# Second head group of a gated convolution: x written by TensorE once, five taps on ScalarE and VectorE, in batches 1 to 6

## Chip, cores and metric

The kernel runs on one core of a Trainium2 chip. The metric is the device time of one launch in microseconds (us). The engines are TensorE (PE; its weight loads are listed apart as PEld), VectorE (DVE), ScalarE (ACT), GpSimd (POOL) and SyncE (SP, which issues the DMAs). PSUM is where TensorE writes; DVE and ACT read it.

## What is computed

Eight batches. In each, eight heads attend to 32 memory slots that are made from k, v and phi; the result, with the heads laid side by side as x (576 rows, 512 channels), goes through a gated convolution.

```python
a = softmax(phi, axis=seq)                       # 576 x 32 weights for each head
k_m, v_m = a.T @ k, a.T @ v                      # 32 x 64 each
attn = softmax(q @ k_m.T / 8, axis=slots)        # 576 x 32
x = attn @ v_m                                   # heads side by side: 576 x 512
gate = sigmoid(sum(conv_w[i] * shift(x, 4 - i) for i in range(5)))   # for each channel
out = (gate * (x @ w_val)) @ w_out
```

## The kernel before, in words

Channels lie on the partitions and sequence positions along the rows, in two halves s of 288 positions. The heads form two groups g of four. The 512 channels are four tiles t of 128; group 0 owns t = 0 and 1, group 1 owns t = 2 and 3. Products against w_val and w_out are made of a high and a low part of each operand (vwH, vwL, pH, pL, hH, hL, woH, woL), three matmuls for each pair.

The steps of one batch b, each a function of that name: `phi_max`, `phi_turn`, `phi_top`, `phi_diag`, `phi_spread`, `phi_lay`, `phi_sub`, `phi_exp` make the softmax over the sequence; `slots`, `slots_inv`, `slots_scale`, `slots_turn`, `slots_place` the memory slots; `scores`, `scores_turn` the scores (PSUM to `st`); `soft_max`, `soft_sub`, `soft_exp`, `soft_sum`, `soft_inv`, `soft_mul` the softmax over the slots; `soft_turn` turns it into `pT`, `soft_high` and `soft_low` split it into pH and pL; `val_rows`, `val_high`, `val_low`, `val_again` fold w_val into the slots' values. `taps(b, g)` multiplies the slots' values by the five tap weights. `conv(b, g)` (L557) multiplies `pT` by these on TensorE, five shifted readings accumulated in PSUM, for both halves and four heads: 40 matmuls with 32 rows and 64 columns of weights, which gives the gate of two channel tiles before the sigmoid. `sigmoid(b, t)` (L572) writes the gate to SBUF. `value(b, s, t)` (L579) makes one channel tile of x @ w_val in six products, `gated(b, s, t)` (L590) multiplies it by the gate into h, `gated_high` and `gated_low` split h, `project(b, s, n)` (L610) makes an output tile in twelve products, `place` copies it out of PSUM, `store` writes it to memory.

In the second half of the positions `conv` puts the heads' channels one place further in the array ("swapped" channels), so that value and project read weights shifted by 64 channels there: `val_again` and `wo_pair` make these copies.

The order of all steps is the text `ORDER` (L38), one word for each step, read from left to right; each engine runs its own instructions in that order and waits for the data of others. A star after a word takes the other of two engines for that step (`pick`, L191): for `phi_sub`, `soft_sub`, `soft_mul`, `soft_low` POOL without a star and DVE with one, for `soft_high` and `gated_high` ACT without and DVE with, for `taps` and `gated_low` POOL without and DVE with.

PSUM is shared out through two pools: four buffers `b` of one bank, for all products but two, and two buffers `cv` of two banks, for `scores`, `conv` and the filler matmuls `warm` at the start. A buffer is written again when its last reader is done.

Of the kernel before, what the change touches and what calls it, by code (L numbers as in the profile page):

```python
# [42 lines left out]
narrow_bits.v.2 narrow_sign.v.2 narrow_size.v.1 narrow_sign.v.0 narrow_round.v.3 narrow_done.v.1 narrow_add.v.0
narrow_round.v.2 narrow_bits.v.3 load_q.0.0 narrow_add.v.2 narrow_sign.v.3 narrow_size.v.0 narrow_size.v.2
narrow_done.v.0 narrow_add.v.3 load_w.o.0 slots.0.0 warm.4 narrow_done.v.2 narrow_size.v.3 load_phi.0.1 slots_inv.0.0
narrow_done.v.3 slots_scale.0.0* load_w.o.1 slots_turn.0.0 taps.0.0* slots_place.0.0 scores.0.0 warm.7 narrow_bits.o.0
narrow_round.o.0 narrow_sign.o.0 load_kv.0.1 phi_max.0.1 narrow_add.o.0 scores_turn.0.0 phi_turn.0.1 warm.7
narrow_round.o.1 soft_max.0.0 narrow_size.o.0 phi_top.0.1 soft_sub.0.0 narrow_bits.o.1 phi_diag.0.1* phi_spread.0.1
warm.9 phi_sub.0.1* load_q.0.1 soft_exp.0.0 soft_sum.0.0 phi_exp.0.1 narrow_done.o.0 load_phi.1 slots.0.1 warm.5
narrow_sign.o.1 wo_high.0 soft_inv.0.0 wo_low.0 slots_inv.0.1 load_w.o.2 soft_mul.0.0* slots_scale.0.1* narrow_add.o.1  # L50
slots_turn.0.1 soft_turn.0.0 slots_place.0.1 val_rows.0 load_w.o.3 soft_high.0.0 phi_max.1 taps.0.1 narrow_size.o.1
scores.0.1 val_high.0.1 soft_low.0.0 load_kv.1.0 scores_turn.0.1 phi_turn.1 val_high.0.0 narrow_round.o.2 soft_max.0.1
conv.0.0 val_again.0.1.vwH val_again.0.0.vwH* phi_top.1 soft_sub.0.1 narrow_round.o.3 val_low.0.0 phi_diag.1*
val_low.0.1 val_again.0.0.vwL soft_exp.0.1 narrow_bits.o.2 phi_spread.1 val_again.0.1.vwL soft_sum.0.1 sigmoid.0.0
load_kv.1.1 soft_inv.0.1 soft_mul.0.1* phi_lay.1 sigmoid.0.1 soft_turn.0.1 phi_sub.1* conv.0.1 soft_high.0.1 load_q.1
soft_low.0.1* phi_exp.1 narrow_bits.o.3 narrow_sign.o.3 value.0.1.2 narrow_sign.o.2 narrow_add.o.3 value.0.0.0
sigmoid.0.2 narrow_done.o.1 value.0.0.1 narrow_add.o.2 slots.1.0 load_phi.2 gated.0.0.0 wo_high.1 gated.0.1.2
gated.0.0.1 narrow_size.o.3 slots.1.1 wo_low.1 slots_inv.1.0 gated_high.0.0.0 wo_pair.0.0 narrow_done.o.3
narrow_size.o.2 value.0.1.0 gated_low.0.0.0 slots_scale.1.0* value.0.0.2 sigmoid.0.3 slots_inv.1.1 gated.0.1.0
wo_pair.1.0 wo_high.3 value.0.0.3 narrow_done.o.2 slots_scale.1.1* wo_low.3 gated.0.0.2 slots_turn.1.0 wo_high.2  # L60
slots_turn.1.1 gated.0.0.3 value.0.1.3 slots_place.1.0 wo_pair.0.1 gated_high.0.0.1* slots_place.1.1 wo_low.2
scores.1.0 gated.0.1.3 scores.1.1 scores_turn.1.0 gated_low.0.0.1 val_rows.1 gated_high.0.1.1 wo_pair.1.1
scores_turn.1.1 value.0.1.1 val_high.1.0 soft_max.1 gated_low.0.1.1 project.0.0.0 val_high.1.1 val_again.1.0.vwH*
load_kv.2.0 val_low.1.0 val_again.1.1.vwH taps.1.1 gated.0.1.1 project.0.0.2 place.0.0.0 val_low.1.1 gated_high.0.1.0
val_again.1.0.vwL soft_sub.1* val_again.1.1.vwL gated_low.0.1.0 project.0.0.1 place.0.0.2 phi_max.2 soft_exp.1
project.0.1.2 load_kv.2.1 taps.1.0* project.0.1.0 place.0.0.1 soft_sum.1 place.0.1.2 project.0.1.3 soft_inv.1
soft_mul.1* store.0.0.0 project.0.1.1 place.0.1.3 soft_turn.1 store.0.1.1 phi_turn.2 load_q.2 soft_high.1* conv.1.0
place.0.1.0 place.0.1.1 phi_top.2 soft_low.1 phi_diag.2* phi_spread.2 sigmoid.1.0 project.0.0.3 load_phi.3 value.1.1.1
phi_lay.2 place.0.0.3 phi_sub.2* value.1.1.0 sigmoid.1.1 store.0.0.1 value.1.0.0 gated.1.1.0 phi_exp.2 store.0.1.0
value.1.0.1 gated.1.1.1 gated.1.0.0 value.1.1.2 gated.1.0.1 phi_max.3 conv.1.1 gated_high.1.1.0 gated_high.1.0.0  # L70
gated_low.1.1.0 slots.2.0 gated_low.1.0.0 sigmoid.1.2 slots.2.1 slots_inv.2.0 load_kv.3.0 sigmoid.1.3 gated.1.1.2
value.1.1.3 slots_scale.2.0* slots_inv.2.1 taps.2.0* slots_scale.2.1* value.1.0.2 gated.1.1.3 taps.2.1 phi_turn.3
gated_high.1.1.1 gated.1.0.2 value.1.0.3 phi_top.3 gated_low.1.1.1 slots_turn.2.1 phi_diag.3* gated.1.0.3
slots_turn.2.0 load_kv.3.1 slots_place.2.1 phi_spread.3 gated_high.1.0.1* slots_place.2.0 scores.2.1 phi_lay.3
gated_low.1.0.1 scores.2.0 phi_sub.3* val_rows.2 project.1.0.0 val_high.2.0 val_high.2.1 val_again.2.0.vwH*
val_again.2.1.vwH load_q.3 val_low.2.0 project.1.1.2 phi_exp.3 val_low.2.1 val_again.2.0.vwL scores_turn.2.0
val_again.2.1.vwL project.1.1.0 scores_turn.2.1 place.1.1.2 place.1.0.0 soft_max.2 project.1.1.3 place.1.1.0
load_phi.4 soft_sub.2* project.1.0.1 place.1.1.3 soft_exp.2 store.1.1.1 project.1.0.3 place.1.0.1 soft_sum.2
store.1.0.0 project.1.0.2 soft_inv.2 soft_mul.2* slots.3.1 place.1.0.2 place.1.0.3 soft_turn.2 store.1.0.1 slots.3.0
soft_high.2* conv.2.1 load_kv.4.0 slots_inv.3.1 soft_low.2 slots_inv.3.0 slots_scale.3.1* phi_max.4 slots_scale.3.0*  # L80
slots_turn.3.0 sigmoid.2.2 slots_turn.3.1 project.1.1.1 taps.3.1 load_kv.4.1 value.2.0.2 slots_place.3.0
slots_place.3.1 sigmoid.2.3 scores.3.0 gated.2.0.2 val_rows.3 place.1.1.1 scores_turn.3.0 phi_turn.4 val_high.3.1
conv.2.0 phi_top.4 val_high.3.0 val_again.3.1.vwH val_low.3.1 phi_diag.4* val_low.3.0 store.1.1.0 val_again.3.1.vwL
val_again.3.0.vwH* val_again.3.0.vwL value.2.0.3 taps.3.0* sigmoid.2.0 value.2.0.1 sigmoid.2.1 gated.2.0.3
gated_high.2.0.1* value.2.1.2 gated_low.2.0.1 value.2.0.0 gated.2.1.2 value.2.1.3 gated.2.0.0 gated.2.0.1 scores.3.1
gated.2.1.3 gated_high.2.0.0 phi_spread.4 load_q.4 scores_turn.3.1 gated_high.2.1.1 gated_low.2.0.0 value.2.1.1
soft_max.3 phi_lay.4 value.2.1.0 gated_low.2.1.1 project.2.0.2 soft_sub.3* gated.2.1.0 project.2.0.1 soft_exp.3
load_phi.5 gated.2.1.1 phi_sub.4* project.2.0.0 gated_high.2.1.0 soft_sum.3 place.2.0.2 gated_low.2.1.0 project.2.0.3
phi_exp.4 soft_inv.3 place.2.0.0 project.2.1.1 place.2.0.3 soft_mul.3* place.2.0.1 store.2.0.0 project.2.1.0
soft_turn.3 store.2.0.1 project.2.1.2 soft_high.3* place.2.1.0 place.2.1.1 store.2.1.0 phi_max.5 conv.3.0 soft_low.3  # L90
place.2.1.2 slots.4.1 sigmoid.3.0 value.3.0.1 slots_inv.4.1 value.3.0.0 slots_scale.4.1* sigmoid.3.1 taps.4.1
value.3.0.2 gated.3.0.0 gated.3.0.1 conv.3.1 gated_high.3.0.0 gated_low.3.0.0 slots.4.0 sigmoid.3.2 sigmoid.3.3
gated.3.0.2 value.3.1.0 slots_inv.4.0 load_kv.5.0 slots_scale.4.0* value.3.1.2 gated.3.1.0 taps.4.0* value.3.1.3
gated.3.1.2 project.2.1.3 gated.3.1.3 gated_high.3.1.1 gated_low.3.1.1 value.3.0.3 place.2.1.3 store.2.1.1
slots_turn.4.0 gated.3.0.3 phi_turn.5 slots_place.4.0 slots_turn.4.1 gated_high.3.0.1* value.3.1.1 load_kv.5.1
slots_place.4.1 phi_top.5 gated_low.3.0.1 scores.4.0 gated.3.1.1 phi_diag.5* scores.4.1 scores_turn.4.0
gated_high.3.1.0 phi_spread.5 gated_low.3.1.0 scores_turn.4.1 project.3.0.0 phi_lay.5 soft_max.4 project.3.1.2
# [580 lines left out]
```

## Time and profile before

| what | value |
|---|---|
| median of three runs | 285.92 us (285.54 to 287.08) |
| the profiled execution | 287.87 us |
| its span, first to last instruction | 286.1 us |
| PE busy | 272.5 us, 95% of the span |
| DVE, ACT, POOL busy | 194.7, 148.8, 107.8 us |
| the chain of work that ended last, by engine | PE 83%, DVE 8%, DMA 4% |

The span is what the rows below divide up; the profiled execution is 1.77 us longer than its span, and 1.95 us longer than the median of the runs.

### The profile page before, as it was taken

Reading aid. Unit: us, or ns where it says so; the run is one execution under the profiler, and the core shown is the slowest. Engines: PE = TensorE matmul, PEld = TensorE weight load, DVE = VectorE, ACT = ScalarE, POOL = GpSimd, SP = SyncE. Lnnn points to the kernel's source line nnn. Section 1 sums busy time; section 2 is a strip of 40 time slices with the busy share of each in tenths; the row PEclk is TensorE's granted clock in tenths of the full one; section 3 lists DMA queues with packets and bytes.
Section 4 is the critical chain, followed back from the end, with each engine's and each line's share of the span. In section 5 each row is a group of like instructions: output and inputs, shape, how many; then the busy total and the mean of one; then the engine's idle time right before and its main releaser. Section 6 shows DMA issues by size and latency. Waiting matters only on the chain.

```text
span 286.1 us, 8415 instructions
## 1 busy us (share of the span) xinstructions
PE 272.5 (95%) x3682; PEld 233.2 (82%) x3682; DVE 194.7 (68%) x287; ACT 148.8 (52%) x262; POOL 107.8 (38%) x96
## 2 busy tenths in 40 slices
...
GB/s 222 353 382 377 309 224 37 134 273 236 322 64 332 266 164 321 10 257 126 165 7 351 157 185 235 89 247 309 183 113 42 32 2 44 82 85 45 41 84 84
DMA packets 13237, 50.00 MB, mean 175 GB/s; under 512 B 1672, under 2 KB 2184, under 8 KB 10256
## 3 DMA queue, kind: packets, MB, share of 16 engines
...
q14 instruction: 8, 0.07, 0.1%
...
## 4 chain that ended last, share of the span: by engine, by line
PE 83%; DVE 8%; DMA 4%; SPq 2%; ACT 1%; issue 0%; POOL 0%; ACTq 0%
PE b L615 34%; PE b L585 17%; PE cv L565 14%; PE b L392 7%; PE cv L438 3%; PE cv L206 2%; DMA raw<-in_w_val_dram 2%; PE b L522 2%; DMA kv<-in_kv_dram 2%; PE b L364 1%; DVE hH L261 1%; DVE hH L254 1%; PE b L422 1%; SPq L313 1%; DVE w_val_sb L286 1%; PE b L336 1%
## 5 line engine op out<-in xcount | busy, mean ns | idle before, releaser
L615 PE MATMUL b<-hL,woH 128*128 128x288 f32 x256 | 76.1, 297 | 0.8 <-DMA kv<-in_kv_dram 0.7
L615 PE MATMUL b<-hH,woL 128*128 128x288 f32 x256 | 75.5, 295 | 0.0
L615 PE MATMUL b<-hH,woH 128*128 128x288 f32 x256 | 75.5, 295 | 0.0
L199 POOL TENSOR_TENSOR hL<-h,hH 128x576 fp32r<-128x576 f32 x32 | 47.1, 1476 | 66.2 <-ACT hH L196 46.0
L594 DVE TENSOR_TENSOR h<-b,gate 128x288 f32<-128x288 f32 x64 | 28.0, 453 | 42.6 <-PE b L585 35.7
L196 ACT COPY o<-b 128x288 f32<-128x288 f32 x64 | 24.6, 399 | 54.9 <-PE b L615 52.9
L615 PEld LDWEIGHTS b<-hL,woH 128*128 128x128 f32 x256 | 48.1, 188 | 3.8 <-POOL hL L199 1.8
L615 PEld LDWEIGHTS b<-hH,woL 128*128 128x128 f32 x256 | 48.1, 188 | 0.0
L615 PEld LDWEIGHTS b<-hH,woH 128*128 128x128 f32 x256 | 48.1, 188 | 0.0
L565 PE MATMUL cv<-pT,taps 32*64 32x288 f32 x1280 | 45.0, 418 | 2.4 <-DVE pT L498 2.4
L565 PEld LDWEIGHTS cv<-pT,taps 32*64 32x64 f32 x1280 | 29.0, 135 | 13.7 <-issue 5.2
L199 POOL TENSOR_TENSOR pL<-pT,pH 128x1152 fp32r<-128x1152 f32 (+1 forms) x8 | 20.9, 2619 | 42.9 <-DVE pH L196 21.5
L585 PE MATMUL b<-pL,vwH 128*128 128x288 f32 x128 | 28.9, 307 | 0.5 <-DVE h L594 0.5
L585 PE MATMUL b<-pH,vwL 128*128 128x288 f32 x128 | 27.3, 295 | 0.0
L585 PE MATMUL b<-pH,vwH 128*128 128x288 f32 x128 | 27.3, 295 | 0.0
L574 ACT ACTIVATE gate<-cv 128x576 f32<-128x576 f32 x32 | 20.2, 652 | 13.5 <-PE cv L565 13.4
L196 ACT CAST hH<-h 128x576 fp32r<-128x576 f32 x24 | 15.9, 672 | 18.9 <-DVE h L594 14.6
L585 PEld LDWEIGHTS b<-pL,vwH 128*128 128x128 f32 x128 | 20.1, 188 | 5.3 <-issue 2.1
L392 PE MATMUL b<-kv,e 128*32 128x129 f32 (+1 forms) x640 | 22.8, 277 | 0.1
L206 PE MATMUL cv<-ident 128*128 128x128 f32 x142 | 20.7, 308 | 1.4 <-POOL ident masks.py:199 1.4
L206 PEld LDWEIGHTS cv<-ident 128*128 128x128 f32 x142 | 19.6, 221 | 2.7 <-POOL ident masks.py:199 1.4
L392 PEld LDWEIGHTS b<-kv,e 128*32 128x32 f32 (+1 forms) x640 | 15.6, 108 | 7.4 <-issue 6.7
...
## 6 DMA issues: line engine op xcount, KB each, us to landing
...
```

The source lines that it names most:

```text
L196: eng.copy(out=out, in_=x) if eng is nc.scalar else eng.tensor_copy(out=out, in_=x)
L199: eng.tensor_tensor(out=out, in0=x, in1=hi.bitcast(F32), op=ALU.subtract)
L206: nc.tensor.matmul(ps[:, i % 2, 0:P], lhsT=ident, rhs=ident, start=True, stop=True)
L254: nc.vector.tensor_scalar(out=a.bitcast(I32), in0=raw[:, :, 1], scalar1=3, scalar2=0x3FFFFFF8, op0=ALU.logical_shift_left, op1=ALU.bitwise ...
L392: nc.tensor.matmul(km[j * M:(j + 1) * M, 0:2 * D + 1], lhsT=e[0:n, g, c, j * M:(j + 1) * M], rhs=x[0:n, c, j, :], start=(c == 0), stop=(c ...
L438: nc.tensor.matmul(sc[j * M:(j + 1) * M, s, 0:HALF], lhsT=live["kvT", b, g][rows, 0, j * M:(j + 1) * M], rhs=live["q", b][rows, g, j, :], ...
L522: nc.tensor.matmul(ps[g][j * M:(j + 1) * M], lhsT=live["kvT", b, g][rows, 1, j * M:(j + 1) * M], rhs=w_val_sb[rows, j, :], start=True, sto ...
L565: nc.tensor.matmul(cv[t][x * D:(x + 1) * D, s, 0:HALF], lhsT=w[rows, i, :], rhs=p[rows, g, s * HALF + i:(s + 1) * HALF + i], start=(i == 0 ...
L574: nc.scalar.activation(out=gt, in_=live["cv", b, t][:, :, 0:HALF], func=AF.Sigmoid)
L585: nc.tensor.matmul(vp[:, 0:HALF], lhsT=a[:, t // PG, n:n + P], rhs=p[:, g, s * HALF:(s + 1) * HALF], start=(i == 0), stop=(i == len(parts) ...
L594: nc.vector.tensor_tensor(out=live["h", b, s, y][:, i], in0=live["vp", b, s, t][:, 0:HALF], in1=live["gate", b, t][:, s], op=ALU.mult)
L615: nc.tensor.matmul(ps[:, 0:HALF], lhsT=w[:, t, n * P:(n + 1) * P], rhs=a[:, t % 2], start=(i == 0), stop=(i == len(parts) - 1))
```

## The change

For group 1 in batches 1 to 6, `conv` and `taps` go. `keep_v` copies the slots' values into a taps tile without multiplying, and `mix` lets TensorE write x itself, for 292 positions of each half (four of them before it), into both `cv` buffers: 8 matmuls in place of 40. `tap(b, t, i)` then makes the convolution from PSUM: i = 0 on ACT (multiply by a weight for each partition, into the gate tile), i = 1 to 4 on DVE (multiply and add into the gate tile, 128 partitions by 576 elements each). `open_gate` is the sigmoid in place. The weights for each partition, `cwP`, are made once by `turn_taps` (10 small matmuls) and `lay_taps`. For that group the channels are no longer moved in the second half, so `val_again` copies half as much, and `value` and `project` read the unshifted weights.

`ORDER` is another text throughout. Counted over it: `phi_sub` of batches 1 to 7 is on POOL where it was on DVE, `soft_high` on ACT where it was on DVE in seven batches, `gated_high` on ACT where DVE had eight of them, all `taps` on POOL, one `place` of each batch on DVE; the filler matmuls are 61, not 71; the loads of w_val's fourth and w_out's tiles come later, those of kv earlier; in batch 7 both convolutions come one after the other at the end of batch 6's projections.

```diff
+VECTOR_CONV = {1, 2, 3, 4, 5, 6}
...
+    def swapped(b, g):
+        return g != G - 1 or b not in VECTOR_CONV
...
+    @step
+    def turn_taps(_):
+        ps = psum.tile([P, 512], F32, name="b", bufs=BUFS["b"])
+        ps = ps[:, 0:KT * PG].rearrange("p (k t) -> p k t", k=KT)
+        for x in range(2):
+            for i in range(KT):
+                nc.tensor.matmul(ps[x * D:(x + 1) * D, i], lhsT=cw_sb[:, 0, i * D:(i + 1) * D],
+                                 rhs=ident[0:H, H - HG + x:H:2], start=True, stop=True)
+        live["cwT"] = ps
+
+    @step
+    def lay_taps(_):
+        high(nc.scalar, cwP, live["cwT"])
...
     def val_again(b, g, n):
+        gs = slice(0, G if swapped(b, G - 1) else G - 1)
         x = live[n, b, g].bitcast(F32)
-        high(pick(nc.gpsimd, nc.scalar), live[n, b, g][:, :, HG * D:], x[:, :, 0:D])
+        high(pick(nc.gpsimd, nc.scalar), live[n, b, g][:, gs, HG * D:], x[:, gs, 0:D])
...
+    @step
+    def keep_v(b):
+        w = work.tile([P, KT, D], F32, name="taps", bufs=BUFS["taps"])
+        high(pick(nc.gpsimd, nc.scalar), w[:, 0], live["kvd", b, G - 1][:, 1, 0])
+        live["taps", b, G - 1] = w
+
+    @step
+    def mix(b):
+        cv = [psum.tile([P, 2, 512], F32, name="cv", bufs=BUFS["cv"]) for _ in range(PG)]
+        for s in range(2):
+            for j in range(HG):
+                rows = slice(j * M, (j + 1) * M)
+                t, x = divmod(j, 2)
+                nc.tensor.matmul(cv[t][x * D:(x + 1) * D, s, 0:PAD + HALF], lhsT=live["taps", b, G - 1][rows, 0, :],
+                                 rhs=pTs[b % 2][rows, G - 1, s * HALF:(s + 1) * HALF + PAD], start=True, stop=True)
+        for j in range(PG):
+            live["cv", b, NP - PG + j] = cv[j]
+
+    @step
+    def tap(b, t, i):
+        x, w = live["cv", b, t][:, :, i:i + HALF], cwP[:, i, t - (NP - PG):t - (NP - PG) + 1]
+        if i == 0:
+            gt = work.tile([P, 2, HALF], F32, name="gate", bufs=BUFS["gate"])
+            nc.scalar.activation(out=gt, in_=x, func=AF.Identity, scale=w)
+            live["gate", b, t] = gt
+        else:
+            gt = live["gate", b, t]
+            nc.vector.scalar_tensor_tensor(out=gt, in0=x, scalar=w, in1=gt, op0=ALU.mult, op1=ALU.add)
+
+    @step
+    def open_gate(b, t):
+        gt = live["gate", b, t]
+        nc.scalar.activation(out=gt, in_=gt, func=AF.Sigmoid)
...
-            n = t % PG * P + s * D
+            n = t % PG * P + (s * D if swapped(b, t // PG) else 0)
...
-        parts = [(w[s], live[a, b, s, t // 2], t) for t in range(NP)
+        parts = [(w[s if swapped(b, t // PG) else 0], live[a, b, s, t // 2], t) for t in range(NP)
                  for w, a in ((woH, "hL"), (woL, "hH"), (woH, "hH"))]
```

**TensorE, around the second group's convolution of batch 2.** L615 (L676 after the change) is project, L392 slots, L565 conv, L611 mix, L422 (L447) slots_turn, L361 phi_turn. Before:

```order
L615 MATMUL b<-hH,woH_83 128x288
L392 MATMUL b<-kv,e 32x129 x40
L565 MATMUL cv<-pT_74,taps 64x288 x40
L422 MATMUL b<-ident,kvd 128x128 x4
L615 MATMUL b<-hL,woH_84 128x288
L615 MATMUL b<-hH,woL_86 128x288
```

In the changed kernel:

```order
L676 MATMUL b<-hH,woH_84 128x288
L611 MATMUL cv<-pT_74,taps 64x292 x8
L361 MATMUL b<-ident,mx 128x128 x2
L447 MATMUL b<-ident,kvd 128x128 x2
L676 MATMUL b<-hL,woH_84 128x288
L676 MATMUL b<-hH,woL_86 128x288
```

The 40 matmuls have become 8, and phi_turn of batch 4, which needs phi_max of batch 4 from DVE, now stands right behind them.

**VectorE, after the softmax of batch 2.** L322, L324 and L325 (L347, L349, L350) are phi_max of batch 4, L594 (L655) gated, L447 (L472) scores_turn, L343 (L368) phi_top, L199 val_low, L550 taps; L207 is here a place and L625 the taps. Before:

```order
L322 TENSOR_TENSOR mx<-e 128x2x2x128
L324 TENSOR_TENSOR mx<-mx 128x256
L325 TENSOR_TENSOR mx<-mx,e 64x256
L594 TENSOR_TENSOR h<-b,gate 128x288
L447 STREAM_TRANSPOSE st<-cv 128x576
L343 TENSOR_REDUCE top<-b 128x2
L199 TENSOR_TENSOR vwL<-b,vwH 128x2x256 x2
L550 TENSOR_TENSOR taps<-cwB,kvd 128x320
```

In the changed kernel:

```order
L347 TENSOR_TENSOR mx<-e 128x2x2x128
L349 TENSOR_TENSOR mx<-mx 128x256
L350 TENSOR_TENSOR mx<-mx,e 64x256
L207 COPY o<-b 128x288
L368 TENSOR_REDUCE top<-b 128x2
L625 SCALAR_TENSOR_TENSOR gate<-cv,cwP,gate 128x576 x8
L655 TENSOR_TENSOR h<-b,gate 128x288 x8
L472 STREAM_TRANSPOSE st<-cv 128x576 x2
```

Eight taps stand between phi_top and the eight gated of batch 2, and all of them ahead of the scores of batch 3.

**GpSimd, batches 1 and 2.** L199 (L210) is soft_low where it writes pL and gated_low where it writes hL, L550 (L576) taps, L196 (L207) val_again, L402 phi_sub. Before:

```order
L199 TENSOR_TENSOR pL<-pT_76,pH 128x1152
L550 TENSOR_TENSOR taps<-cwB,kvd 128x320
L199 TENSOR_TENSOR hL<-h,hH 128x576 x4
L199 TENSOR_TENSOR pL<-pT_74,pH 128x1152
L196 CAST vwH<-vwH 128x2x64
L196 CAST vwL<-vwL 128x2x64 x2
```

In the changed kernel:

```order
L210 TENSOR_TENSOR pL<-pT_74,pH 128x1152
L576 TENSOR_TENSOR taps<-cwB,kvd 128x320
L210 TENSOR_TENSOR hL<-h,hH 128x576 x4
L402 TENSOR_TENSOR e<-e,mxa 128x1280
L207 CAST vwL<-vwL 128x64 x2
L210 TENSOR_TENSOR pL<-pT_76,pH 128x1152
```

phi_sub, which was DVE's, now stands in POOL's queue between gated_low and the next soft_low.

## Rows read from the trace of the kernel before

**Rows 1.** Busy time in two stretches (columns in its first line)

```profile
core 0: us, PE busy (x) PEld busy (x) DVE busy (x) ACT busy (x) POOL busy (x), PEclk, DMA share, GB/s
...
100.00:130.00 30.00, 30.00 (x437) 25.14 (x436) 24.36 (x35) 15.41 (x30) 10.84 (x9) 1.00 0.51 181
220.00:253.00 33.00, 33.00 (x459) 28.33 (x458) 18.75 (x29) 15.05 (x28) 11.33 (x10) 1.00 0.12 46
```

**Rows 2.** The chain of work that ended last: start us, us, what (L565 conv)

```profile
41.90 4.47 PE cv L565 x80
...
71.67 0.22 PE b L336 x2
71.88 2.61 PE cv L565 x80
74.50 0.64 PE b L364 x4
...
88.87 0.44 PE b L422 x4
...
90.08 1.13 PE cv L438 x32
91.21 0.86 PE b L522 x16
...
109.33 1.59 PE b L615 x12
110.91 0.79 PE b L585 x6
...
136.96 1.37 PE b L392 x40
```

**Rows 3.** Groups by line: shapes, xcount, busy us, mean ns, idle before

```profile
L574 ACT ACTIVATE gate<-cv 128x576 f32<-128x576 f32 x32 | 20.2, 652 | 13.5 <-PE cv L565 13.4
...
L199 DVE TENSOR_TENSOR vwL<-b,vwH 128x512 fp32r<-128x512 f32 x16 | 10.4, 682 | 5.3 <-ACT vwH L196 5.3
...
L411 ACT ACTIVATE kvd<-b,ri 128x256 f32<-128x256 f32 x16 | 7.6, 475 | 13.9 <-DVE ri L401 13.7
...
L196 ACT COPY kvT<-b 128x256 f32<-128x256 f32 x16 | 5.4, 372 | 3.2 <-PE b L422 3.1
```

**Rows 4.** DVE's phi_max of batches 6 and 7: start us, us, engine, line

```profile
164.90 0.68 DVE L322 TENSOR_TENSOR mx<-e 128x512 f32<-128x512 f32 x1
165.62 2.76 DVE L324 TENSOR_TENSOR mx<-mx 128x256 f32<-128x256 f32 x1
168.41 0.42 DVE L325 TENSOR_TENSOR mx<-mx,e 64x256 f32<-64x256 f32 x1
...
199.76 0.43 DVE L324 TENSOR_TENSOR mx<-mx 128x256 f32<-128x256 f32 x1
```

**Rows 5.** DVE from scores_turn to soft_turn of batch 5, columns as rows 4

```profile
183.60 1.45 DVE L447 STREAM_TRANSPOSE st<-cv 128x576 f32<-128x576 f32 x2 [0.68 <-PE cv L438]
...
186.64 1.34 DVE L462 TENSOR_REDUCE mm<-st 128x36 f32<-128x1152 f32 x1
...
188.26 1.37 DVE L469 TENSOR_TENSOR st<-st,mm 128x1152 f32<-128x1152 f32 x1
190.87 1.35 DVE L480 TENSOR_REDUCE ss<-st 128x36 f32<-128x1152 f32 x1 [1.24 <-ACT st L474]
...
192.88 1.36 DVE L493 TENSOR_TENSOR st<-st,ss 128x1152 f32<-128x1152 f32 x1
194.27 1.38 DVE L498 STREAM_TRANSPOSE pT<-st 128x1152 f32<-128x1152 f32 x1
```

**Rows 6.** POOL's soft_low of batch 4, columns as rows 4

```profile
165.06 3.04 POOL L199 TENSOR_TENSOR pL<-pT,pH 128x1152 fp32r<-128x1152 f32 x1 [10.85 <-DVE pH L196]
```

**Rows 7.** PE's clock before and in the convolution of batch 0, columns as rows 1

```profile
40.00:42.00 2.00, 0.10 (x2) 0.13 (x5) 1.93 (x4) 1.83 (x5) 0.00 (x0) 1.00 0.01 5
42.00:44.00 2.00, 2.00 (x36) 2.00 (x43) 2.00 (x3) 1.97 (x3) 0.00 (x0) 0.52 0.00 0
```

More of the change, by code (lines that the diff above doesn't have):

```diff
@@ L43 @@
[L43 to L97, printed above, removed]
@@ new lines @@
+warm.9 soft_sub.0.0* phi_sub.0.1* soft_exp.0.0 load_q.0.1 soft_sum.0.0 phi_exp.0.1 soft_inv.0.0 slots.0.1 warm.5
+load_phi.1 narrow_bits.o.0 narrow_round.o.0 narrow_sign.o.0 slots_inv.0.1 narrow_add.o.0 soft_mul.0.0*
+slots_scale.0.1* load_w.o.1 slots_turn.0.1 narrow_done.v.3 taps.0.1 slots_place.0.1 narrow_size.o.0 scores.0.1
+soft_turn.0.0 val_rows.0 warm.5 load_w.o.2 narrow_done.o.0 soft_high.0.0 phi_max.1 val_high.0.0 soft_low.0.0 wo_high.0
+load_w.o.3 narrow_round.o.1 scores_turn.0.1 phi_turn.1 val_again.0.0.vwH* wo_low.0 val_high.0.1 phi_top.1 conv.0.0
@@ new lines @@
+project.2.0.2 gated_low.2.1.1 phi_lay.4 scores_turn.3.1 soft_max.3 val_rows.3 phi_sub.4 place.2.0.2 soft_sub.3*
+project.2.0.0 val_high.3.0 val_high.3.1 load_phi.5 val_low.3.0 soft_exp.3 project.2.1.0 place.2.0.0* val_again.3.0.vwL
+val_low.3.1 project.2.0.3 val_again.3.1.vwL phi_exp.4 soft_sum.3 project.2.1.2 val_again.3.1.vwH* soft_inv.3
+place.2.0.3 val_again.3.0.vwH* store.2.0.1 soft_mul.3* place.2.1.0 slots.4.0 soft_turn.3 slots.4.1 load_kv.5.0
+phi_max.5 soft_high.3 mix.3 place.2.1.2 soft_low.3 slots_inv.4.0 phi_turn.5 tap.3.3.0 project.2.0.1 slots_inv.4.1
@@ new lines @@
+soft_inv.4 store.3.0.1 soft_mul.4* project.3.1.2 place.3.1.0 soft_turn.4 slots.5.0 place.3.1.2 phi_max.6 soft_high.4
+mix.4 load_kv.6.0 soft_low.4 phi_turn.6 slots_inv.5.0 tap.4.2.0 project.3.1.1 phi_top.6 slots_scale.5.0* tap.4.2.1
+tap.4.3.0 tap.4.2.2 slots_turn.5.0 phi_diag.6* project.3.1.3 taps.5.0 slots_place.5.0 tap.4.2.3 place.3.1.1
+store.3.1.0 tap.4.2.4 value.4.1.2 place.3.1.3 tap.4.3.1 open_gate.4.2 store.3.1.1 value.4.0.2 tap.4.3.2 value.4.0.3
+tap.4.3.3 value.4.1.3 gated.4.1.2 scores.5.0 tap.4.3.4 slots.5.1 gated.4.0.2 open_gate.4.3 scores_turn.5.0 value.4.0.0
@@ L175 @@
     cwB = const.tile([P, G, KT * D], F32, name="cwB")
+    cwP = const.tile([P, KT, PG], F32, name="cwP")
     pick_head = const.tile([H, H, M], F32, name="pick_head")
```

135 lines of the change are left out of this document (90 added, 45 removed).

## Prediction

> **What bounds the kernel now.** I read the busy time by stretches first. From 66 us on TensorE is busy for all of every stretch at a granted clock of 1.00, which is its upper level of 2.4 GHz, while DVE takes 24.4 of 30 us in one stretch and 18.8 of 33 in another, POOL about a third [rows 1]. Then the chain of work that ended last: from 65 us to the end it is a row of PE pieces that follow each other without a gap, and the convolutions are among them, 2.61 us each, two in a batch [rows 2]. So every microsecond of PE work that goes after 66 us comes off the time, as long as no other engine makes PE wait. Before 66 us it is otherwise: there DVE's long list of weight conversions and the first two softmaxes set the pace, and PE fills its waits with matmuls that compute nothing.
>
> **What goes.** Six convolutions leave PE, 6 x 2.61 us. Each is replaced by mix: 8 matmuls of 32 rows, seen as 16 pieces. The convolution's 80 pieces take 2.61 us, so 16 of that kind take 0.52; scores, the other product with 288 columns and four heads side by side, takes 1.13 us for 32 pieces, 0.57 for 16 [rows 2]. I take 0.56 (four columns more). The saving is 6 x 2.05 = **12.3 us**, all of it on the path. The ten small matmuls of turn_taps lie in the head, ahead of 14 filler matmuls, and cost nothing there; val_again's smaller copies and the missing taps free POOL and ACT, which are not on the chain.
>
> **What comes, on DVE and ACT.** No row shows a multiply-and-add of 128 x 576 from PSUM. The nearest is val_low, two operands, one in PSUM, 128 x 512: 0.682 us [rows 3]. Scaled by columns that is 0.77, from which I take the price of a tap; less than 0.68 is not to be had for more columns, and the upper end is 0.91, if a scalar for each partition adds the 0.10 that separates slots_scale (scaled, 0.475) from a plain copy of the same size (0.372) on ACT [rows 3], rounded up. Eight taps are 6.2 us of DVE in each of six batches, 37 in all. The first tap on ACT is a sigmoid's 0.652 plus that 0.10, 0.75; open_gate costs what the sigmoid cost. DVE gives up phi_sub, soft_high and smaller steps for them. In its fullest stretch it had 24.4 of 30 us [rows 1], 22.9 in the 28.2 that PE will need for a batch (below); 6.2 more less what it gives up stays under 29.1, so DVE comes close to PE and, on the mean, not past it. But between the softmax of one batch and the next its work is in series with PE's, and that must be walked.
>
> **The ring.** From the end of soft_turn of batch 2 to that of batch 3 the changed order runs: on DVE phi_max of batch 4, 0.68 + 0.43 + 0.42 = 1.5 us where POOL leaves it alone [rows 4]; then phi_turn on PE, which stands right behind mix, so that PE is past it at 1.9. Then PE to the end of the scores of batch 3: three projects, eight values, one convolution, two slots_turn, two scores: 4.8 + 6.3 + 2.6 + 0.4 + 1.1 = 15.3 us [rows 2]. In that time DVE does phi_top, a place, the eight taps and gated; both `cv` buffers must be read out before the remaining convolution can start, at 2.8 + 6.2 = 9.0 us against PE's arrival at 9.3. So the taps are covered with 0.3 us to spare at 0.77, and cost 0.8 at 0.91. Then DVE alone: two scores_turn 1.45, soft_max 1.34, soft_sub 1.37, instead of the wait for the exponential two val_low and a place (1.8), soft_sum 1.35, the reciprocal 0.66 (from the end of soft_sum to soft_mul's start), soft_mul 1.36, soft_turn 1.38 [rows 5], with handoffs 10.9. The ring is 1.9 + 15.3 + 10.9 = 28.1. One thing lengthens it. phi_sub now stands in POOL's queue. What POOL does there to DVE is seen where soft_low ran for 3.04 us [rows 6]: the second step of phi_max, begun 0.6 us later, took 2.76 us, up to POOL's end, where it takes 0.43 with POOL idle [rows 4]. By columns phi_sub (1280 against 1152) takes 2.9 to 3.4 us on POOL. In batch 3 it begins about 1 us before soft_sub is due, which then waits some 2.1. The ring becomes 30.2.
>
> PE's own work from mix to mix in that loop is 28.2 us (eight projects 12.7, eight values 6.3, the convolution, two slots 2.7, mix, scores, val_rows and the small products 3.9). So PE waits. The same walk for the other loops, PE's work against the ring: batches 1 to 2, 29.8 against 29.0; 3 to 4, 28.5 against 29.9; 4 to 5, 28.2 against 29.9; 5 to 6, 26.4 against 27.1; 6 to 7, 29.4 against 29.1. The loops differ by how many projects stand in them and by how far phi_sub falls in with the softmax. Waits: 0, 1.2 (PE comes 0.8 late out of the loop before), 1.4, 1.7, 0.7, 0, together **5.0 us** given back. The bounds of this term: 0, where POOL lets DVE pass and the handoffs are shorter by half a microsecond, and about 9, with taps at 0.91 in every loop.
>
> **The head.** Up to the second soft_turn of batch 0 DVE has about 1 us less in its list: two val_low (1.4) and a taps step leave this stretch, a soft_sub of half size (0.7) joins it. The second convolution of batch 0 ran 4.47 us there, where the others take 2.61 [rows 2]: after PE had done next to nothing from 40 to 42 us its granted clock was 0.52, the lower level of 1.2 GHz, from 42 to 44 [rows 7]. In the new order its wait is shorter if DVE is sooner, and the 1.86 us may or may not go. I take 1.9 us off for the head, with 0 and 3 as ends. The tail holds the same work as before, eight values, a convolution and eight projects behind the last soft_turn, and I take it at nothing either way.
>
> **The sum** against the profiled execution: 287.87 - 12.3 + 5.0 - 1.9 = 278.7. The median of the runs lay 1.95 below it, so **276.7 us**.
>
> **The rivals.**
> *Cover holds.* The rings close without waits: POOL's work does not fall in with DVE's, PE stays full. For it: in the kernel before, DVE had such meetings with POOL [rows 6, 4] and PE never waited for it after 66 us. Against: the rings above leave no room. 287.87 - 12.3 - 1.9 - 1.95 = 271.7.
> *The clock falls.* PE waits behind soft_turn and again behind phi_max, with 0.56 us of mix between them. The one wait of that size in the trace was followed by half the clock, which cost 1.86 us [rows 2, 7]. In the four loops with a wait that is 7.4 more: 284.1, a gain of 0.6%; with six such falls 287.9. Against: most of the waits I find are shorter than that one of 2.4 us.
> *POOL holds DVE in every loop*, the one on the other side. A whole phi_sub (3.0) ahead of soft_sub in the five loops that have one, where I counted 4.9 in all, adds 9.4; and phi_max is held by soft_low as in batch 4, 2.3 more in the three loops whose phi_turn stands right behind mix, adds 6.9. All of it gives 293.0. It is slower than before once 9.2 of these 16.3 us come about. For it: each of these meetings has its row; against: soft_high is now ACT's, so soft_low starts 1.2 us after soft_turn, when phi_max is nearly through. The Trainium skill has a rule on this ("SBUF — State Buffer", Who interferes with whom): a DVE instruction with two operands in SBUF and a GpSimd one that reads SBUF shut each other out whole, and the first to issue wins; by that rule the taps, with x in PSUM, are never held, but soft_sub and phi_max are, for as long as POOL's instruction lasts. The trace agrees for phi_max (2.76 against 0.43 us), and shows no tap.
> *The head gives back.* The fourth tile of w_val and all of w_out load later, and PE or POOL could wait for them; with the head 4 us later instead of 1.9 earlier: 282.6.
>
> **How the numbers follow.** Forecast with its own bounds (272 to 281): 0.50. Cover holds: 0.18. Clock falls: 0.17, of which 0.08 stays faster by over 0.5%, 0.06 within it, 0.03 slower. POOL holds DVE: 0.09, of which 0.07 slower. Head: 0.06. So faster by over 0.5% (1.4 us, about what a measurement of this kernel can tell from no change) 0.82, within it 0.08, slower 0.10. The range runs from 271 to 285: it takes in the forecast, the cover that holds, the head and the milder falls of the clock, and leaves out some 0.18.
>
> **What would show it.** Right: conv's group with 800 pieces instead of 1280 and mix with 96 at about 35 ns each; PE idle behind soft_turn and phi_max for 4 to 6 us in all between 66 us and the end, at clock 1.00; taps of 0.7 to 0.8 us; soft_sub stretched where phi_sub runs. Wrong, if the taps take 0.9 us or more and the remaining convolution waits for them; if the stretches behind the waits show a clock near 0.5; if PE is full throughout; or if the head ends more than 2 us later.

## The result: 2.8 us faster where 9.2 was forecast

| | before | after | ratio (95%) |
|---|---|---|---|
| set of the result | 285.73 us | 282.94 us | 0.9891 (0.9854 to 0.9929) |
| chip 9 | 287.83 | 281.09 | 0.9765 (0.9725 to 0.9806) |
| chip 1 | 287.54 | 281.58 | 0.9800 (0.9751 to 0.9850) |
| chip 1, later | 287.88 | 282.70 | 0.9799 (0.9710 to 0.9888) |

The times are medians of all runs; the ratios leave out slow runs, of which three kernels below had one or two in ten. The direction was right and 282.94 us lies in the range, but the gain is 2.8 us in the first set and 5.2 to 6.7 in the others, against a forecast of 9.2. The profiled execution took 282.87 us, its span 281.1.

The sets differ by TensorE's clock in the head of the program. Executions of the kernel before with a mean granted clock of 0.992 or 0.994 took 285.5 to 286.6 us, those with 0.982 took 287.1 to 289.3; after, 279.1 and 281.0 at 0.994, and 281.8 to 282.4 at 0.982. Like with like the gain is about 6 us. In the first set three of the four times of before lie at this short end (285.3 to 285.9), and those of after, at 0.976 to 0.982, do not.

### The profile page after: what moved, and what is told of

Same layout as the page of the kernel before. It is cut to its first block, busy times and chain, and to the rows that moved or that the text cites. A ratio compares the mean times of both kernels' runs of the same rounds, so it can differ in the third digit from the quotient of the medians.

```text
span 281.1 us, 7710 instructions
## 1 busy us (share of the span) xinstructions
PE 266.7 (95%) x3298; PEld 225.4 (80%) x3298; DVE 201.1 (72%) x312; ACT 164.1 (58%) x289; POOL 130.0 (46%) x103
## 4 chain that ended last, share of the span: by engine, by line
PE 81%; DVE 15%; ACT 2%; issue 1%; POOL 0%; POOLq 0%
PE b L676 31%; PE b L646 18%; PE cv L591 10%; PE b L417 7%; PE cv L217 5%; PE cv L463 3%; DVE st L494 2%; PE cv L611 2%; DVE mx L349 2%; PE b L547 2%; DVE st L472 2%; DVE mm L487 1%; DVE mx L350 1%; PE b L389 1%; PE b L361 1%
## 5 line engine op out<-in xcount | busy, mean ns | idle before, releaser
L210 POOL TENSOR_TENSOR hL<-h,hH 128x576 fp32r<-128x576 f32 x32 | 47.6, 1495 | 72.2 <-ACT hH L207 58.1
L676 PE MATMUL b<-hL,woH 128*128 128x288 f32 x256 | 76.8, 300 | 0.9 <-DVE vwL L210 0.9
L676 PE MATMUL b<-hH,woL 128*128 128x288 f32 x256 | 75.5, 295 | 0.0
L676 PE MATMUL b<-hH,woH 128*128 128x288 f32 x256 | 75.4, 294 | 0.0
L655 DVE TENSOR_TENSOR h<-b,gate 128x288 f32<-128x288 f32 x64 | 27.7, 449 | 39.3 <-PE b L646 22.0
L676 PEld LDWEIGHTS b<-hL,woH 128*128 128x128 f32 x256 | 48.1, 188 | 6.6 <-POOL hL L210 2.6
L676 PEld LDWEIGHTS b<-hH,woL 128*128 128x128 f32 x256 | 48.1, 188 | 0.0
L676 PEld LDWEIGHTS b<-hH,woH 128*128 128x128 f32 x256 | 48.1, 188 | 0.0
L207 ACT COPY o<-b 128x288 f32<-128x288 f32 x56 | 21.7, 398 | 35.4 <-PE b L676 33.6
L625 DVE SCALAR_TENSOR_TENSOR gate<-cv,cwP,gate 128x576 f32<-128x576 f32 x48 | 38.2, 814 | 4.7 <-ACT gate L621 3.7
L210 POOL TENSOR_TENSOR pL<-pT,pH 128x1152 fp32r<-128x1152 f32 (+1 forms) x9 | 22.1, 2458 | 30.2 <-ACT pH L207 30.2
L207 ACT CAST hH<-h 128x576 fp32r<-128x576 f32 x32 | 21.1, 672 | 19.9 <-DVE h L655 19.9
L591 PE MATMUL cv<-pT,taps 32*64 32x288 f32 x800 | 28.7, 420 | 2.9 <-DVE vwL L210 2.5
L646 PE MATMUL b<-pL,vwH 128*128 128x288 f32 x128 | 29.5, 311 | 0.0
L591 PEld LDWEIGHTS cv<-pT,taps 32*64 32x64 f32 x800 | 17.4, 136 | 11.1 <-issue 5.1
L417 PE MATMUL b<-kv,e 128*32 128x129 f32 (+1 forms) x640 | 22.7, 277 | 0.0
L402 POOL TENSOR_TENSOR e<-e,mxa 128x1280 f32<-128x1280 f32 x7 | 21.0, 2994 | 2.6 <-ACT mxa L207 2.6
L217 PEld LDWEIGHTS cv<-ident 128*128 128x128 f32 x122 | 18.6, 240 | 3.7 <-POOL ident masks.py:199 1.4
## 6 DMA issues: line engine op xcount, KB each, us to landing
q<-in_q_dram SPq DMA_DIRECT2D x2, 576.0 KB, 10.1
```

What stands on the lines that cost most here:

```text
L207: eng.copy(out=out, in_=x) if eng is nc.scalar else eng.tensor_copy(out=out, in_=x)
L210: eng.tensor_tensor(out=out, in0=x, in1=hi.bitcast(F32), op=ALU.subtract)
L217: nc.tensor.matmul(ps[:, i % 2, 0:P], lhsT=ident, rhs=ident, start=True, stop=True)
L402: eng.tensor_tensor(out=t, in0=t, in1=mxa.unsqueeze(2).to_broadcast(list(t.shape)), op=ALU.subtract)
L417: nc.tensor.matmul(km[j * M:(j + 1) * M, 0:2 * D + 1], lhsT=e[0:n, g, c, j * M:(j + 1) * M], rhs=x[0:n, c, j, :], start=(c == 0), stop=(c ...
L591: nc.tensor.matmul(cv[t][x * D:(x + 1) * D, s, 0:HALF], lhsT=w[rows, i, :], rhs=p[rows, g, s * HALF + i:(s + 1) * HALF + i], start=(i == 0 ...
```

## The profile after

Two stretches of the kernel after, to be read against [rows 1]:

```profile
core 0: us, PE busy (x) PEld busy (x) DVE busy (x) ACT busy (x) POOL busy (x), PEclk, DMA share, GB/s
100.00:130.00 30.00, 29.84 (x321) 25.88 (x320) 24.19 (x34) 18.29 (x32) 14.49 (x11) 1.00 0.50 174
220.00:253.00 33.00, 33.00 (x412) 28.82 (x408) 21.43 (x34) 19.39 (x33) 14.21 (x11) 1.00 0.09 34
```

TensorE is as full as before, at the upper level of its clock. All that made it wait from 73 us to the end is one row (what waited, for what, us in all, times, longest):

```profile
PE b L676 <- DVE vwL L210: 0.2, 1, 0.2
```

So the 5 us of waits that the prediction gave back are not there. Three rows of TensorE in the loop from mix of batch 2 to that of batch 3 (start us, us, line, pieces): mix, the remaining convolution, the scores.

```profile
103.86 1.21 PE L611 MATMUL cv<-pT,taps 32*64 32x292 f32 x16
...
112.73 2.68 PE L591 MATMUL cv<-pT,taps 32*64 32x288 f32 x80
...
119.73 1.20 PE L463 MATMUL cv<-q,kvT 64*32 64x288 f32 x32
```

Here is the first gap: 16 pieces of mix take as long as 32 of the scores. Groups of DVE and POOL (busy us, mean ns, idle before):

```profile
L625 DVE SCALAR_TENSOR_TENSOR gate<-cv,cwP,gate 128x576 f32<-128x576 f32 x48 | 38.2, 814 | 4.7 <-ACT gate L621 3.7
...
L494 DVE TENSOR_TENSOR st<-st,mm 128x1152 f32<-128x1152 f32 (+1 forms) x8 | 17.1, 2133 | 0.1
...
L402 POOL TENSOR_TENSOR e<-e,mxa 128x1280 f32<-128x1280 f32 x7 | 21.0, 2994 | 2.6 <-ACT mxa L207 2.6
```

A tap costs 0.81 us; soft_sub (L494), 1.37 us in [rows 5], has a mean of 2.13, since POOL's phi_sub (L402) shuts it out. The second gap is in the head. TensorE at phi_turn of batch 2, DVE's soft_sub of batch 1, POOL's phi_sub of batch 2, and the clock in the stretches around the first of them:

```profile
57.43 0.44 PE L361 MATMUL b<-ident,mx 128*128 128x128 f32 x2 [1.60 <-DVE mx L350]
...
62.41 3.71 DVE L494 TENSOR_TENSOR st<-st,mm 128x1152 f32<-128x1152 f32 x1
...
61.96 2.94 POOL L402 TENSOR_TENSOR e<-e,mxa 128x1280 f32<-128x1280 f32 x1 [0.23 <-ACT mxa L207]
```

```profile
56.00:58.00 2.00, 0.57 (x3) 0.41 (x4) 2.00 (x3) 0.00 (x0) 1.09 (x1) 1.00 0.67 152
58.00:60.00 2.00, 2.00 (x11) 2.00 (x11) 1.83 (x5) 1.81 (x4) 1.05 (x1) 0.58 0.95 190
60.00:62.00 2.00, 2.00 (x15) 1.40 (x22) 1.34 (x2) 0.51 (x3) 1.77 (x3) 0.57 0.98 380
```

TensorE waits 1.6 us for phi_max of batch 2, its clock is at the lower level for the values behind that wait, and soft_sub waits out phi_sub. Mix of batch 1 begins at 72.9 us, where the second group's convolution of batch 1 began at 71.8 before. That difference alone says little, since the place moves from execution to execution: 71.8 and 73.1 in two traces of the kernel before, 71.4 to 73.1 in four of the kernel after. What does differ is the work that TensorE has done by then: 36 pieces of project fewer (4.9 us) and 80 of slots more (2.7).

## The experiments

The theory from the two traces: TensorE still sets the time from 73 us on; mix is dearer than forecast because of the way it uses the array; the new order loses time in the head. The rival: the ring of DVE and POOL (softmax, taps, phi_sub) has become the bound, and TensorE's saving is lost to it.

**Mix over all eight tiles.** In the kernel, `t, x = divmod((j - s) % HG, 2)` stands in mix for `divmod(j, 2)`.

> One index is changed in mix: in the second half of the positions each head writes the other half of the columns, as conv does it. The second group's channels then lie in a wrong order there; the amount of work is the same. Theory: mix costs 1.14 us and not 0.56 because only four of the array's eight 32 by 64 tiles are used, four pieces at a time and not eight, and TensorE still bounds the time from 73 us on. Then mix takes about 0.6 and the time falls by 6 x 0.55 = 3.3 us, to about 279.6. Rival: the ring of DVE and POOL is by now as long as TensorE's work; then mix gets shorter, TensorE waits for it, and the time falls by less than 1.5 us.

Measured: 280.58 us, ratio 0.9761 (0.9685 to 0.9837), in a set without the kernel after; mix takes 0.75 us. A second set had the kernel after beside it:

> The changed kernel with mix over all eight tiles of the array, once more, now beside the changed kernel itself: mix 0.75 us from first to last piece and not 1.21, TensorE waits some 1.4 us in the loops, and the time is 1.5 to 2 us below the changed kernel's, not 2.8 (the second half's channels of that group are in a wrong order).

Measured: 280.85 us, where the kernel after took 281.58, so 0.7 us less and not 1.5 to 2; from mix of batch 1 to the last product both traces have 203.6 us against 205.1, 1.45 us less. TensorE at mix of batches 2 and 3 in the first set's trace, and its waits from 74 us on:

```profile
103.02 0.75 PE L611 MATMUL cv<-pT,taps 32*64 32x292 f32 x16
104.12 0.41 PE L361 MATMUL b<-ident,mx 128*128 128x128 f32 x2 [0.35 <-DVE mx L350]
...
132.91 0.75 PE L611 MATMUL cv<-pT,taps 32*64 32x292 f32 x16
```

```profile
PE b L361 <- DVE ri L424: 0.9, 2, 0.6
PE b L361 <- DVE mx L350: 0.3, 1, 0.3
```

The price is explained: 0.46 us of each mix is the unused half of the array. Of the 2.8 us in six batches 1.3 go into waits at phi_turn, which stands right behind mix and needs phi_max, begun when soft_turn ends (the release by `ri` is the last of several that phi_turn needs). So theory and rival each hold in half of the program. The kernel after, at mix of batch 3:

```profile
133.82 1.22 PE L611 MATMUL cv<-pT,taps 32*64 32x292 f32 x16
```

From mix to mix the loop of batch 2 takes 29.96 us there and 29.89 here; the next two change by 0.05 us or less (29.52 to 29.47, 29.77 to 29.78). In these three the ring is as long as TensorE's work in the kernel after already, and the rival is right. The loops of batches 1 and 5 and the end of the program shrink by the whole 0.44 to 0.46 us.

**Are DVE's taps behind these waits?** The kernel above, without `tap.b.t.1` to `tap.b.t.3` in the order.

> As the one before it, and with three of the four taps of DVE left out for each tile (so the convolution is not the reference's): DVE has 36 instructions of 0.81 us less, 29 us. Theory (with mix at 0.75 us the ring of DVE and POOL is the longer one, by 1.4 us over the loops): TensorE's waits behind 73 us go, and the stretch from mix of batch 1 to the last product takes 202.3 us, 2.7 less than in the changed kernel and 1.3 less than with all taps. Rival (something else than DVE's length makes those waits): the stretch stays at 203.6.

Measured: 281.33 us, ratio 0.9807 (0.9724 to 0.9890), from mix of batch 1 to the end 203.55 us. The waits from 74 us on:

```profile
PE b L358 <- DVE ri L421: 0.9, 2, 0.6
PE b L358 <- DVE mx L347: 0.3, 1, 0.3
PE b L673 <- DVE vwL L207: 0.2, 1, 0.2
```

The same waits at phi_turn with 29 us less on DVE: the expectation failed. The taps are covered and no part of the ring. What closes it is the way from soft_turn over phi_max to phi_turn, and from there over the scores to the next soft_turn; its piece at phi_turn is hidden behind mix when mix takes 1.21 us.

**The convolution with channels in place.** The new order with the old convolution (next experiment), in which the second group's convolution is put on four tiles:

```diff
-                    t, x = divmod((j - s) % HG, 2)
+                    t, x = divmod((j - s * swapped(b, g)) % HG, 2)
```

> The changed kernel's order with the convolution on TensorE in all batches, and with the second group's channels left in place in batches 1 to 6: the convolution's 80 pieces there then use four of the array's eight 32 by 64 tiles, as mix does, and not all eight. Theory (what doubled mix's price is the number of tiles in use): these six convolutions take 5.1 us each and not 2.68, the others stay at 2.68, and the time is 6 x 2.4 = 14.5 us above that of the same order with moved channels. Rival (mix is dear for another reason, its first pieces or its 292 columns): they stay near 2.7 us, and so does the time.

Measured: 306.51 us, against 291.49 for the same order with moved channels on this chip. The two convolutions of batch 2, the second group's first:

```profile
108.13 5.08 PE L587 MATMUL cv<-pT,taps 32*64 32x288 f32 x80
...
120.88 2.68 PE L587 MATMUL cv<-pT,taps 32*64 32x288 f32 x80
```

One index doubles it: 80 pieces in 5.08 us, and 15.0 us in the time where 6 x 2.40 = 14.4 come from the rows. From that place of batch 1 to the last product the traces differ by the same 14.4 (228.2 us against 213.8): work that is added to TensorE there lengthens the time by as much. In the records, pieces on eight tiles start eight at a time every 0.24 us, those of mix four at a time every 0.25. The Trainium skill ("TensorEngine Tiling (Array Packing)", Tiling Modes) lists eight independent tiles of 32 x 64, each tied to its input and output partitions; the rows agree, and a head whose channels stay in place has the same tile in both halves.

**The order without mix.** The kernel after with `taps.b.1`, `conv.b.1` and the two sigmoids where keep_v, mix and the last taps stood, and `VECTOR_CONV = set()`.

> The changed kernel's order of the steps, but with the convolution on TensorE in all batches: taps and conv stand where keep_v and mix stood, the sigmoid where the last tap stood, channels moved in the second half as before. If TensorE bounds the time from 73 us on, conv for mix adds 6 x (2.61 - 1.14) = 8.8 us: 291.7, and the new order by itself would be some 6 us slower than the old one. If DVE's ring bounds it, which loses 37 us of taps here, the time rises by less than 5 us: under 288.

Measured: 290.61 us, ratio 1.0116 (1.0048 to 1.0185). Again, beside the kernel after:

> The changed kernel's order with the convolution on TensorE as before, once more, now beside the changed kernel on one chip. If the time splits into the order and mix as the traces say, it lies 3 us above the kernel before (the order alone) and 8.8 us above the changed kernel (six times 2.68 - 1.21).

> The changed kernel on the same chip: 281 to 283 us, 5 to 6 us under the kernel before.

Measured: 291.49 us, ratio 1.0105 (1.0058 to 1.0151), and 282.70 for the kernel after. Waits of TensorE from 73 us on in the first of the two:

```profile
PE b L672 <- DVE vwL L206: 0.2, 1, 0.2
```

This divides the result. The order alone costs 3.0 to 3.3 us by the ratios (the first expectation had said 6, the second 3). TensorE is full behind 73 us, so the loss is made in the head. In the traces it is work that the head leaves for later: from the second group's convolution of batch 1 to the last product this kernel takes 213.8 us and the kernel before 211.2, 2.6 more. Mix in that order gives 8.8, six times 2.68 - 1.21, and the traces agree (213.8 against 205.1). Together 5.5 to 5.8, about what like executions show.

**The order of before, with mix.**

> The kernel before's order in full, with mix where the second group's convolution stood, keep_v where its taps stood, and the five taps and open_gate where its two sigmoids stood, in batches 1 to 6. If TensorE's saving of 8.8 us needs no other order, the time is 277 on the scale where the kernel before takes 285.7. If DVE, which keeps phi_sub and half of gated_high here and gets 37 us of taps, becomes the bound, as its 24.4 of 30 us plus 6.4 in the fullest stretch suggest, TensorE waits in most loops and the time is at or above the kernel before's, 286 to 295.

Measured: 333.24 us, ratio 1.1576 (1.1528 to 1.1624), well beyond the worse expectation. TensorE's longest waits:

```profile
PE b L647 <- DVE ri L425: 13.3, 2, 7.1
PE b L647 <- DVE h L656: 11.8, 3, 6.6
PE b L647 <- DVE vwL L211: 7.6, 2, 7.4
```

In the old order the taps stand ahead of small DVE steps that TensorE needs for the next batch: in the longest wait for `ri`, up to 93.4 us, DVE runs six taps. Among these waits the granted clock falls too: its mean is 0.918, against 0.98 in the kernel after, with 0.57 from 90 to 98 us and 0.50 from 121 to 131. The 3 us of the new order save some 50, the clock's part included.

**phi_sub back on DVE.** `phi_sub.1*` to `phi_sub.7*`.

> Only phi_sub of batches 1 to 7 goes back from POOL to DVE, where it was before the change. Theory (TensorE is full, so what POOL does to DVE is hidden from 73 us on): the time stays within 1 us of 282.9, though soft_sub falls from 2.3 to 1.4 us. Rival (POOL's phi_sub, which shuts DVE's soft_sub out, makes the ring and the head long): DVE gets 7 x 1.4 us more and is shut out 6 x 1 us less in the rings, and the head ends about 2 us sooner, so 280 to 281.

Measured: 288.17 us, ratio 1.0018 (0.9978 to 1.0057), 4 to 7 us worse than the kernel after by the ratios (its set had no kernel after). Both expectations failed. Groups of DVE, and waits of TensorE:

```profile
L494 DVE TENSOR_TENSOR st<-st,mm 128x1152 f32<-128x1152 f32 (+1 forms) x8 | 12.6, 1577 | 0.0
...
L402 DVE TENSOR_TENSOR e<-e,mxa 128x1280 f32<-128x1280 f32 x7 | 11.2, 1596 | 1.9 <-ACT mxa L207 1.9
```

```profile
PE b L676 <- DVE vwL L210: 2.1, 3, 1.1
...
PE b L646 <- DVE vwL L210: 0.9, 1, 0.9
```

soft_sub loses most of its stretch, 4.5 us in all, but DVE carries 11.2 us more in the softmax. TensorE waits for val_low behind it: from mix of batch 1 to the last product it takes 208.2 us against 205.1. Mix of batch 1 begins at 74.7 us, later than in all four traces of the kernel after. POOL's lock costs DVE less than the work that POOL takes over.

**The head.** Four kernels tried to win it back, and each came out slower than the kernel after on its chip. First, phi_max of batch 2 behind `soft_exp.1`, the rest of batch 2's phi steps and slots behind `mix.1`, `project.0.1.0` and `.2` ahead of `soft_turn.1`:

> The changed kernel with one stretch of its order put later: phi_max of batch 2 behind soft_exp of batch 1 (where the kernel before had it), the rest of batch 2's sequence softmax and its slots behind mix of batch 1, and two projections of batch 0 ahead of soft_turn in their place. Theory (the head loses its time because batch 2's phi_max, phi_turn and phi_sub stand in front of batch 1's softmax): mix of batch 1 begins at 70 to 71 us instead of 72.9, soft_sub of batch 1 takes 1.4 instead of 3.7, and the time falls by 2 to 3 us against the changed kernel. Rival (DVE's list of conversions sets the head, and what is put later is paid for later): mix begins sooner, but TensorE waits in the loop behind it, and the time stays within 1 us.

Measured: 283.08 us, ratio 0.9837 (0.9790 to 0.9883), where the kernel after took 281.09.

> The changed kernel once more, timed beside the other kernels of this set. If its gain belongs to the kernel, it lies again about 2.8 us (ratio 0.989) under the kernel before, mix takes 1.2 us from first to last piece, and mix of batch 1 begins within 1 us of 72.9.

The kernel after kept mix at 1.22 us and its place at 72.89, but its gain was 6.7 us and not 2.8. The first kernel:

```profile
70.97 1.22 PE L611 MATMUL cv<-pT,taps 32*64 32x292 f32 x16
...
79.38 2.81 PE L417 MATMUL b<-kv,e 128*32 128x129 f32 x80 [1.61 <-ACT e L407]
...
103.82 1.21 PE L611 MATMUL cv<-pT,taps 32*64 32x292 f32 x16
```

Mix of batch 1 begins 1.9 us sooner and mix of batch 2 where it was (103.82 against 103.86): paid for later, as the rival has it, though at 2.0 us above the kernel after the time lies outside the rival's 1 us too. Second, one projection ahead instead of two:

> The changed kernel with batch 2's sequence softmax put later, as in the earlier run, but with one projection of batch 0 ahead of soft_turn instead of two, and three behind mix. In the earlier run mix of batch 1 waited 1.1 us for the second projection, and TensorE waited 1.6 us for phi_exp of batch 2 later. If the head's loss is a matter of where TensorE's work is put, both go and the time falls 1 to 1.5 us below the changed kernel's; if the chain through DVE and POOL up to mix of batch 2 sets it, mix of batch 2 begins at 103.8 again, or at 102.5 in the best case, and the time is within 1 us of the changed kernel's.

Measured: 284.62 us, ratio 0.9894 (0.9811 to 0.9976), where the kernel after took 282.70; mix of batch 2 at 106.96, later than either forecast. Third, the kernel before's words up to `soft_turn.1`, then the rest:

> The kernel before's own order up to soft_turn of batch 1 (its loads, conversions, filler matmuls, and phi_sub of batch 1 on DVE), then the changed kernel's order for all that is left, with mix. Theory (the new order's head costs 3.7 us: it ends 1.1 us later and has done 2.6 us less of TensorE's work): mix of batch 1 begins at about 71.8, what is left takes TensorE some 1.5 us less than in the changed kernel, and the time is 2.5 us below the changed kernel's. Rival: as for the kernel with batch 2's softmax put later, within 1 us.

Measured: 284.69 us, ratio 0.9893 (0.9843 to 0.9943), where the kernel after took 281.09: outside theory and rival again. Mix of batch 1 at 71.37, of batch 2 at 105.59. TensorE's longest waits from 60 us to mix of batch 2, of the second kernel and of the third:

```profile
PE b L417 <- ACT e L407: 1.6, 1, 1.6
PE b L676 <- DMA woH<-woH: 1.6, 1, 1.6
PE b L676 <- DMA woL<-woL: 0.8, 1, 0.8
```

```profile
PE b L418 <- ACT e L408: 3.0, 1, 3.0
PE b L677 <- DMA kv<-in_kv_dram: 0.7, 1, 0.7
```

In all three, slots of batch 2 wait for the exponential behind phi_sub (rows L417 and L418), by then behind mix of batch 1; in the second kernel projections wait for woH and woL ahead of it too. Behind the 3.0 us wait of the third kernel the granted clock is 0.50 from 80 to 82 us. Fourth, fillers, `warm.8` ahead of `phi_turn.1` and `warm.6` ahead of `phi_turn.2`:

> The changed kernel with filler matmuls in two of TensorE's waits in the head: eight in front of phi_turn of batch 1 (it waits 2.5 us there for phi_max) and six in front of phi_turn of batch 2 (1.6 us). Behind both waits the changed kernel's profile shows the granted clock at 0.5 for 3.4 us. Theory (what the head loses is in good part this clock): both stretches stay at 1.00, the first convolution of batch 0 takes 2.7 us and not 3.9, the values behind phi_turn of batch 2 0.8 us and not 1.4, and the median falls by 1 to 2 us to about 281. Rival (DVE's list sets the head): the clock stays up, but the time stays within 0.5 us.

> The changed kernel, timed on one chip beside the three that follow: 280.9 to 284.8 us as so far, its times in the order of the mean granted clock of the execution (0.994 the shortest, 0.969 the longest).

Measured: 286.27 us, ratio 0.9959 (0.9915 to 1.0003), against 281.58 and 0.9800 for the kernel after. Fillers and phi_turn of batch 1, and the stretch:

```profile
33.65 3.78 PE L218 MATMUL cv<-ident 128*128 128x128 f32 x16 [3.15 <-DVE st L473]
37.22 0.63 PE L362 MATMUL b<-ident,mx 128*128 128x128 f32 x2
```

```profile
34.00:38.00 4.00, 4.00 (x26) 3.67 (x33) 0.11 (x1) 0.00 (x0) 0.00 (x0) 0.50 0.93 352
```

The first eight fillers need a `cv` buffer that scores_turn empties, so they waited themselves and then ran at half the clock in front of phi_turn. The other six did what they were put in for: with them ahead of phi_turn of batch 2 the granted clock stayed at 1.00 from 60 to 64 us. As the first eight failed, the clock's price is not measured here, but the chain has no slack at the first: phi_turn of batch 1 came 4 us late, and so did mix of batch 1 (75.4 against 71.4).

**The kernel before once more.**

> The kernel before once more, to see what of its profile is the same in each execution. If the low clock behind TensorE's wait at 40 to 42 us belongs to the kernel, the second convolution of batch 0 takes about 4.5 us again and the span is 286.1; if it belongs to that one execution, the convolution takes 2.6 to 2.7 us, and span and time are 1.9 us shorter, which is about what the profiled execution stood above the median.

Measured: 289.15 us, span 287.4, and behind the same wait:

```profile
43.15 4.49 PE L565 MATMUL cv<-pT,taps 32*64 32x288 f32 x80 [2.42 <-DVE pT L498]
```

The low clock was there again; the span was not. From the second group's convolution of batch 1 to the last product both executions took 211.2 us; they differ only ahead of it, 71.8 and 73.1. The kernel after shows the same. From 10 to 14 us, first in the trace of the result, then in the one beside the fillers:

```profile
10.00:14.00 4.00, 4.00 (x23) 3.98 (x23) 3.34 (x5) 1.88 (x4) 2.24 (x2) 0.57 0.99 333
...
10.00:14.00 4.00, 4.00 (x54) 3.88 (x56) 3.31 (x5) 2.22 (x6) 2.24 (x2) 1.00 1.01 307
```

With the lower level there (0.57) mix of batch 1 begins at 72.89 us, without it at 71.38; from there on both take 205.1.

## Why the prediction was wrong in size

- **What bounds the kernel: right, in one direction.** Behind 73 us work added to TensorE lengthens the time one to one (14.4 us, 8.8 us). Of the 2.8 us that eight tiles took off mix, only 1.45 came off: with so little less work the ring binds in three loops.
- **What goes, 12.3 us: mis-sized, 8.8 measured.** The failed step is "16 of that kind take 0.52", and with it the 0.56 taken for mix. The two rows it was worked out from, convolution and scores [rows 2], use eight tiles at once, and mix uses four. The kernel showed it: `(j - s) % HG` in conv had become `j` in mix. By the same measure mix is 1.21 us and the convolution 2.68, a saving of 1.47 a batch and not 2.05. Of the 0.58 lacking 0.46 is the unused half of the array; the other 0.12 is that even 16 pieces on eight tiles take 0.75, more than a fifth of 80.
- **A tap: right**, 0.81 us where 0.77 was taken, 0.80 to 0.82 in all 48, not stretched in the 21 that ran beside an instruction of POOL on operands in SBUF, as the rule of the Trainium skill in the prediction ("SBUF — State Buffer", Who interferes with whom) has it; that page's lock on soft_sub shows too (3.71 us).
- **The ring, 5.0 us: wrong, 0.2 measured.** The walk through the ring was good: 30.2, 29.9 and 29.9 us forecast for the loops of batches 2 to 4, and 29.90, 29.67 and 29.79 from one soft_turn's end to the next in the kernel with mix over eight tiles, where TensorE waits for the ring. Beside POOL's phi_sub, soft_sub took 3.1, 2.1, 1.8 and 2.8 us in four loops. What failed was the other side of the difference, "PE's own work ... is 28.2 us". By the records that loop holds 29.8 us: mix 0.6 more, and project 13.4 instead of 12.7 and value 6.7 instead of 6.3, because the rows' times for one were multiplied, without the longer start where one product follows another of a different kind. In the five loops up to batch 6 TensorE's work was 1.0 to 1.6 us more than forecast. Differences of 0.7 to 2.0 us between two sums near 29 do not bear such an error. The same loop of before, read as one stretch of the trace, would have warned: it is 28.2 us from one second group's convolution to the next and holds the same products, only without the two slots (2.7). With these and the prediction's own 2.05 off for mix it makes 28.9, with the measured 1.47 off 29.5.
- **The head, -1.9 us: wrong in sign, +3.0 to +3.3 measured.** The walk stopped at the second soft_turn of batch 0. Up to soft_turn of batch 1 the new order also holds batch 2's phi_turn, phi_sub and half of its slots, and its phi_max sooner (before, phi_max stood behind soft_exp of batch 1); three of batch 0's projections have gone behind it. That these steps cost the 3 us is argued from the two traces. The kernel that put them back behind mix was no faster, and the cause stays open, as does whether another order could have this back; the three tried, and the fillers, did not.
- **The 1.95 us from the profiled execution to the median** were taken off both sides. Where and how often the clock falls in the head differs from execution to execution, and one such fall moved everything behind it by 1.5 us (72.89 against 71.38), so that this was no constant. It is the likely cause of the distance from 2.8 us in the first set to 5.2 and more in the others; the clocks of the first set's timed runs of before were not recorded, so this is argued from their times.
- **The sum:** 9.2 forecast - 3.5 (mix) + 4.8 (ring) - 5 (head) = 5.5, near the 6 us of like executions. That 282.94 us fell into the range owes something to luck: 4.8 us too many hid as much of the 8.5 too few.
- **The rivals.** "Cover holds" came true for the ring, by 0.1 us or less in three loops, and of the prediction's signs of being wrong "PE is full throughout" was seen. The clock did not fall behind 73 us, as TensorE did not wait there; where it did wait (the old order, the third head) the clock fell. POOL's lock came as described and was hidden; the 9.4 us of that rival do not follow from its terms (5 x 3.0 - 4.9 is 10.1), and nothing hangs on them. "The head gives back" was the right place with the wrong mechanism.
